# Attention, experts and MLP in one kernel: thresholds on ScalarE and GpSimd, router tables by 108 lanes, steps moved behind the branch

## The chip, the cores and the metric

The kernel runs on one core of a Trainium2 chip. The metric is the device time of one execution in microseconds; the median of several is compared. The core's engines each work off a list of their own: TensorE (PE; its weight loads are shown as PEld), VectorE (DVE), ScalarE (ACT), GpSimd (POOL), and SyncE (SP), which issues most transfers. They wait for one another through semaphores.

## What is computed

Three stages follow one another. Attention has 4 x 8 heads, 576 positions, head width 64, and keeps only scores near each row's maximum. Its output, 2304 tokens of 512, goes to a mixture of 8 experts with one expert per token, and then through an MLP.

```python
    scores = scale * np.matmul(q, k.transpose(0, 1, 3, 2))
    thresh = np.max(scores, axis=-1, keepdims=True) - tau
    scores = np.where(scores >= thresh, scores, -1000000000.0)
    scores = scores - np.max(scores, axis=-1, keepdims=True)
    attn = np.exp(scores)
    attn = attn / (np.sum(attn, axis=-1, keepdims=True) + 1e-09)
    return np.matmul(attn, v).astype(np.float32)
...
    logits = x @ w_gate
    e_idx = np.argmax(logits, axis=1)
...
    eom = 1.0 / (1.0 + np.exp(-(x @ w_output_gate)))
...
        h = np.maximum(x[mask] @ w1[e], 0.0)
        ye = h @ w2[e]
        out[mask] = gate_w[mask, None] * eom[mask, e, None] * ye
...
    h = x @ w_in
    g = np.maximum(0.01 * h, h)
    return (g @ w_out).astype(np.float32)
```

## The kernel before

**Attention** (the first 340 us) works through 16 pairs of heads. A pair P has 9 tiles of 128 rows by 576 columns. Each tile runs: scores on TensorE (L443, into `ps`), row maximum on VectorE (L452, `nm`), then a threshold of one number per row (L456, `th` = tau's share minus `nm`), the exponential on ScalarE (L462, `e`), the mask on VectorE (L470, `em`, which compares the scores with `th`, multiplies with `e` and sums into `rr`), transposes on TensorE (L499, and L535 for the last columns), their evictions (L228 on ScalarE, L230 on VectorE), and the products with the values (AV: L578 in steps of two instructions, L584 as the last step of each half). At a pair's end come L619, L636 and L649 to L651 with the evictions L624, L654 and L662 (`lg`, the gates' logits). For a later pair, GpSimd swaps key halves by DMA (L391, L392) and splits the raw q and k in two parts (casts L290, subtractions L295; `srk`, `srq`), which TensorE transposes (L319, L345). The evictions of a small part of q are `qz`.

**The router** (class `Router`) runs once per batch, that is, after every four pairs: `batch` finds each token's expert (L795 to L821), its rank within the expert (L858 to L880) and its weight (L823 to L846). `choose`, late in attention, picks the expert with most tokens ("star") and makes the list of its first 216 tokens, so that `prefix` can begin its first matrix (L1460) while the last batch is routed. `entries` turns ranks into table entries (`lo`, `sides`): for batches 0 to 2 together after `choose`, for batch 3 alone. `tables` makes the inverse table, the experts' order and the lists of tokens per expert (`gidx`), the flag L1116, and `starts` the first row of each expert.

**The branch.** Each engine loads the flag (L1982) and compares (L1983); the branch body, for experts with more tokens than their window holds, isn't entered with these inputs. Steps that the planner has placed later than `st.t_over` stand behind the branch in each engine's list, the others ahead of it.

**Experts and dense stage.** From 360 us on, eight windows of at most `CAPS` tokens (and the second matrix of the prefix's 216) are computed with weights that arrive by SP's transfers and are split into two parts: casts L1559 and subtractions L1564. L1661 and L1669 and L1675 make the first matrix and its evictions, L1702 the second; L1630 transposes gathered tokens. From 622.9 us the MLP (L1836, L1862) fills TensorE.

The order in each engine's list is made by a list scheduler, `Plan`: each step has an engine (or several to choose from), a cost, a priority and an earliest time, and instructions are put out in planned order. The numbers `st.w_*` are the priorities of the kinds of steps within a pair.

## Time and profile before

| | |
|---|---|
| median of 3 runs | 1031.69 us (1031.01 to 1036.69) |
| profiled execution | 1034.34 us, span 1032.6 us |
| busy share of the span | PE 95%, PEld 81%, DVE 64%, ACT 48%, POOL 25% |
| mean granted TensorE clock | 0.980 of full speed |
| bytes read from and written to HBM | 88.39 MB, 23.31 MB |

A row of a timeline gives start, duration, engine, line, operation, output and inputs with shapes, and in brackets how long the engine stood idle before it, and what released it. A table by stretches gives each engine's busy time within a stretch. A granted clock of 1.00 is TensorE's 2.4 GHz, half of it 1.2 GHz. TensorE's instructions overlap, so what counts is the distance between their starts.

### The profile page before, as it was taken

Reading aid. Unit: us, or ns where it says so; the run is one execution under the profiler, and the core shown is the slowest. Engines: PE = TensorE matmul, PEld = TensorE weight load, DVE = VectorE, ACT = ScalarE, POOL = GpSimd, SP = SyncE. Lnnn points to the kernel's source line nnn. Section 1 sums busy time; section 2 is a strip of 40 time slices with the busy share of each in tenths; the row PEclk is TensorE's granted clock in tenths of the full one; section 3 lists DMA queues with packets and bytes.
Section 4 is the critical chain, followed back from the end, with each engine's and each line's share of the span. In section 5 each row is a group of like instructions: output and inputs, shape, how many; then the busy total and the mean of one; then the engine's idle time right before and its main releaser. Section 6 shows DMA issues by size and latency. Waiting matters only on the chain. (4 is left out here: it accounts for less than half of the span.)

```text
span 1032.6 us, 17029 instructions
## 1 busy us (share of the span) xinstructions
PE 982.6 (95%) x6126; PEld 836.8 (81%) x6126; DVE 658.5 (64%) x1279; ACT 498.0 (48%) x944; POOL 260.2 (25%) x328
## 2 busy tenths in 40 slices
PE   6999999999999799899999999999999999999994
PEld 6777767767776699789999997888888888888884
DVE  7888988898889558998888886533223222322321
ACT  6777767767766255544554644423222322322321
POOL 3533223323211244464337532000100100100000
PEclk9999999999999989899999999999999999999997
DMA  5432423431312597887989877200200200100000
GB/s 140 127 86 71 129 59 85 127 73 41 103 25 96 166 260 261 296 269 241 324 298 320 289 241 232 83 1 12 70 1 1 81 1 1 42 20 1 11 31 22
DMA packets 66876, 122.22 MB, mean 118 GB/s; under 512 B 15776, under 2 KB 33184, under 8 KB 66272
## 3 DMA queue, kind: packets, MB, share of 16 engines
q1 hardware_dynamic: 60368, 100.43, 30.5%
q0 software_dynamic: 6416, 20.63, 7.3%
q8 instruction: 50, 0.82, 0.3%
q14 instruction: 42, 0.34, 0.2%
HBM read 88.39 MB, written 23.31 MB: 108 GB/s over the span
## 5 line engine op out<-in xcount | busy, mean ns | idle before, releaser
L1862 PE MATMUL ps<-arena 128*128 128x512 f32 x864 | 207.4, 390 | 2.3 <-ACT arena L1559 2.3
L1836 PE MATMUL ps<-arena 128*128 128x512 f32 (+1 forms) x960 | 208.1, 368 | 0.0
L1836 PEld LDWEIGHTS ps<-arena 128*128 128x128 f32 x960 | 168.7, 188 | 30.8
L1862 PEld LDWEIGHTS ps<-arena 128*128 128x128 f32 x864 | 161.3, 188 | 35.7 <-ACT arena L1559 2.7
L1847 DVE TENSOR_TENSOR dw<-ps,dw 128x512 f32<-128x512 f32 (+1 forms) x80 | 50.9, 638 | 160.7 <-ACT dw L1843 160.6
L1702 PE MATMUL ps<-arena 128*128 128x216 f32 (+7 forms) x864 | 129.8, 309 | 3.8 <-ACT arena L1669 2.2
L1843 ACT ACTIVATE dw<-ps 128x512 f32<-128x512 f32 (+1 forms) x80 | 44.4, 556 | 183.4 <-PE ps L1836 183.4
L1661 PE MATMUL ps<-arena 128*128 128x400 f32 (+7 forms) x768 | 117.9, 313 | 10.7 <-DVE arena L1675 4.1
L1702 PEld LDWEIGHTS ps<-arena 128*128 128x128 f32 x864 | 124.0, 194 | 4.8 <-ACT arena L1669 2.5
L1661 PEld LDWEIGHTS ps<-arena 128*128 128x128 f32 x768 | 113.9, 194 | 13.6 <-DVE arena L1675 5.1
L452 DVE TENSOR_REDUCE nm<-ps 128x1 f32<-128x576 f32 x144 | 107.0, 753 | 22.4 <-PE ps L443 21.1
L470 DVE SCALAR_TENSOR_TENSOR em<-ps,th,e 128x576 f32<-128x576 f32 x144 | 115.1, 811 | 4.6 <-ACT e L462 2.3
L462 ACT ACTIVATE e<-ps,nm 128x576 f32<-128x576 f32 x144 | 105.7, 749 | 17.0 <-DVE nm L452 12.2
L1891 POOL DMA_INDIRECT out_dram<-sm,oidx x18 | 18.0, 999 | 367.4 <-ACT sm L1885 334.2
L1564 DVE TENSOR_TENSOR arena<-dw,arena 128x512 fp32r<-128x512 f32 (+1 forms) x80 | 52.0, 650 | 91.6 <-PE ps L1862 75.8
L443 PE MATMUL ps<-k,qt 128*128 128x288 f32 x512 | 101.6, 326 | 7.2 <-DVE em L470 6.0
L228 ACT COPY eta<-ps 128x512 f32<-128x512 f32 (+1 forms) x159 | 86.2, 545 | 42.3 <-PE ps L499 41.0
L1559 ACT CAST arena<-raw 128x1024 fp32r<-128x1024 f32 x82 | 84.7, 1048 | 43.1 <-DMA raw<-in_moe_w_dram 33.3
L1564 POOL TENSOR_TENSOR arena<-raw,arena 128x1024 fp32r<-128x1024 f32 x30 | 77.0, 2568 | 82.8 <-ACT arena L1559 69.1
L443 PEld LDWEIGHTS ps<-k,qt 128*128 128x128 f32 x512 | 75.8, 196 | 25.0 <-DVE em L470 10.6
L1564 DVE TENSOR_TENSOR arena<-raw,arena 128x1024 fp32r<-128x1024 f32 x54 | 78.2, 1451 | 26.7 <-ACT arena L1559 21.6
L499 PE MATMUL ps<-ident,em 128*128 128x128 f32 x576 | 89.8, 281 | 1.3 <-DVE em L470 0.7
(236 smaller groups left out, 1161.5 us busy)
## 6 DMA issues: line engine op xcount, KB each, us to landing
raw<-in_moe_w_dram SPq DMA_DIRECT2D x72, 512.0 KB
k<-k POOLq DMA_DIRECT2D x30, 304.0 KB
dw<-in_moe_w_in_dram SPq DMA_DIRECT2D x16, 512.0 KB
wf<-cv SPq DMA_DIRECT2D x32, 256.0 KB
dw<-in_moe_w_out_dram SPq DMA_DIRECT2D x16, 512.0 KB
raw<-wf SPq DMA_DIRECT2D x16, 512.0 KB
rk<-in_k_dram SPq DMA_DIRECT2D x16, 256.0 KB
rq<-in_q_dram SPq DMA_DIRECT2D x16, 256.0 KB
```

The costliest lines, as they stand in the source:

```text
L228: nc.scalar.copy(out=out, in_=in_)
L443: nc.tensor.matmul(out=s[:, c, :], lhsT=lhs, rhs=T[kk, P][:, off + c * HALF:off + (c + 1) * HALF], start=(m == 0), stop=(m == 2 * len(ops) ...
L452: nc.vector.tensor_reduce(out=T["nm", n], in_=T["sc", n], axis=AX.XY, op=ALU.max, negate=True)
L462: nc.scalar.activation(out=T["e", n].rearrange("p (a c) -> p a c", a=2), in_=T["sc", n], func=AF.Exp, bias=T["nm", n][:, 0:1], scale=1.0,)
L470: nc.vector.scalar_tensor_tensor(out=T["em", P, t][:, h, :].rearrange("p (a c) -> p a c", a=2), in0=T["sc", n], scalar=T["th", n][:, 0:1], ...
L499: nc.tensor.transpose(out=bank(o)[:, c * 128:(c + 1) * 128], in_=T["em", P, t][:, h, 64 * h + c * 128:64 * h + (c + 1) * 128], identity=ident,
L1559: nc.scalar.copy(out=out, in_=in_)
L1564: (nc.vector if o.eng == "dve" else nc.gpsimd).tensor_tensor(out=out, in0=in0, in1=in1, op=ALU.subtract)
L1661: nc.tensor.matmul(out=bank(o)[:, 0:n], lhsT=w[:, wi, 128 * f:128 * f + 128], rhs=xx[:, xi, c, :], start=(c == 0 and i == 0), stop=(c == K ...
L1702: nc.tensor.matmul(out=bank(first, d)[:, 0:n], lhsT=w[:, wi, k0:k0 + 128], rhs=hx[:, xi, :], start=(f == 0 and i == 0), stop=(f == 7 and i ...
L1836: nc.tensor.matmul(out=bank(o)[:, 0:n], lhsT=w[:, wi, c, 128 * c2:128 * c2 + 128], rhs=y[:, c, 0:n], start=(k == 0), stop=(k == 3 * KD - 1),)
L1862: nc.tensor.matmul(out=bank(first, t), lhsT=g[:, gi, 128 * t:128 * t + 128], rhs=w[:, wi, c2, :], start=(f == 0 and k == 0), stop=(f == FF ...
```

## The change

1. The thresholds are computed on ScalarE (an activation Identity with scale -1 and tau's share as bias) or on GpSimd; none on VectorE.
2. The tables have 108 lanes (`LANES`) and 6 places for each expert in place of 128 and 4. `entries` runs in every batch: `ge`, `ges`, `lane` and `lo` on VectorE, and `eqj`, `eqab` and two `sides` on GpSimd for batches 0 to 2. The chosen expert's ranks aren't shifted any more; `left` takes its first 216 tokens out of the table at the end. `choose` loses its steps `mine`, `low` and `shift`. Tokens are gathered by 108 rows, 25 gathers in place of 23.
3. The token lists of the experts after the first, the starts and the rest of the last gate come behind the branch; `CAPS[2]` is 324 in place of 336.
4. The planner's numbers are others, and `st.t_over` is 2.2. By the orders of the two kernels, thresholds go from 47 on DVE and 97 on POOL to 85 on ACT and 59 on POOL; 14 of 16 `qz` evictions go from ACT to DVE.

```diff
+LANES = PRE // 2
+
+CAPS = [400, 368, 324, 320, 296, 272, 248, 216]

...
-                (nc.vector if o.eng == "dve" else nc.gpsimd).tensor_tensor(
-                    out=T["th", n], in0=ntau, in1=T["nm", n], op=ALU.subtract
-                )
+                if o.eng == "act":
+                    nc.scalar.activation(out=T["th", n], in_=T["nm", n], func=AF.Identity, bias=ntau[:, 0:1], scale=-1.0)
+                else:
+                    nc.gpsimd.tensor_tensor(out=T["th", n], in0=ntau, in1=T["nm", n], op=ALU.subtract)
...
-            th = pl.add(("dve", "pool"), (0.07, 0.15), thresh, [m], n + st.w_th, label="th")
+            th = pl.add(("act", "pool"), (0.18, 0.15), thresh, [m], n + st.w_th, label="th")
...
-    J = 4
+    J, JW = 6, 4
...
+        entered = self.entries(pl, b, ranked, one_hot, prio)
         if end:
...
+        self.before += entered
...
             nc.vector.tensor_tensor(
-                out=self.lo[:, 5 * b:5 * b + 5, :], in0=self.it.unsqueeze(1).to_broadcast([128, 5, 128]),
-                in1=X["rlo"][:, 5 * (b - b0):5 * (b - b0) + 5].unsqueeze(2).to_broadcast([128, 5, 128]), op=ALU.is_equal,
+                out=ge, in0=rk.unsqueeze(2).to_broadcast([128, 5, J + 1]),
+                in1=self.edge.unsqueeze(1).to_broadcast([128, 5, J + 1]), op=ALU.is_ge,
+            )
+            nc.vector.tensor_reduce(out=s, in_=ge[:, :, 1:J + 1], axis=AX.X, op=ALU.add)
+            nc.vector.scalar_tensor_tensor(out=lane, in0=s, scalar=-float(LANES), in1=rk, op0=ALU.mult, op1=ALU.add)
+
+        def low(o):
+            nc.vector.tensor_tensor(
+                out=self.lo[:, g, :], in0=self.it.unsqueeze(1).to_broadcast([128, 5, 128]),
+                in1=X["lane"].unsqueeze(2).to_broadcast([128, 5, 128]), op=ALU.is_equal,
             )
...
+            V = nc.vector if end else nc.gpsimd
+            eq, ab = w.tile([128, 5, J], F32, name="eqj"), w.tile([128, 5, 2, J], BF16, name="eqab")
...
+        hi = pl.add("dve" if end else "pool", 0.4, high, [pt], prio, label="en")
+        out = [pl.add("dve", 0.8, low, [pt], prio, label="en")]
...
-        m = pl.add("dve", 2.0, mine, [s, ranked], pr, label="ch")
-        ls = [pl.add("dve", 0.8, lambda o, b=b: low(o, b), [m], pr, label="ch") for b in range(NB)]
...
+            self.table(ia_)
+            a, b = t("tsa", (E, J)), self.w.tile([128, E, J], F32, name="tsb")
+            for x, i, m in ((a, 0, self.rest), (b, 2, self.star)):
...
-        a = add("dve", 1.2, lambda o: tokens(o, 1, E), [a])
-        return add("dve", 1.1, starts, [a])
+        self.others, self.starts = lambda o: tokens(o, 1, E), starts
+        return add("dve", 0.9, fits, [a])
...
+    others = pl.add("dve", 1.2, R.others, [], -13, at=free, label="tb")
+    starts = pl.add("dve", 1.3, R.starts, [], 5, at=free, label="tb")
...
-        last = pl.add(eng, cost, f, [last], 6, lat=4.0 if eng == "sp" else 0.0, label="gate")
+        last = pl.add(eng, cost, f, [last], 30, lat=4.0 if eng == "sp" else 0.0, at=20.0, label="gate")
...
-    st.w_s, st.w_m, st.w_th, st.w_x, st.w_kk, st.w_t, st.w_te = -0.39, -0.27, -4.42, -1.71, -7.74, 2.69, -4.82
-    st.w_l = [1.2, 6.62]
...
+    st.w_s, st.w_m, st.w_th, st.w_x, st.w_kk, st.w_t, st.w_te = -0.83, -9.42, -28.19, 3.88, -7.61, 2.26, -14.75
+    st.w_l = [-0.74, 7.52]
...
-    st.t_over = 3.0
...
+    st.t_over = 2.2
```

How the instructions stand now, at the places of which the prediction speaks. First VectorE in the pair that begins the first batch, before: L795 to L805 are steps of the gate's choice, L452 and L470 row maximum and mask.

```order
170 L795 TENSOR_TENSOR scr<-lg 128x160
171 L797 TENSOR_TENSOR lg_1618<-scr 128x80
172 L470 SCALAR_TENSOR_TENSOR em,rr_175<-ps,th,e 128x576
173 L452 TENSOR_REDUCE nm<-ps 128x1
174 L801 TENSOR_REDUCE m<-lg_1618 128x5
175 L456 TENSOR_TENSOR th<-ntau,nm 128x1
176 L805 TENSOR_TENSOR eq<-lg_1618,m 128x40
```

After: L800 to L810 are those steps, L454 and L473 row maximum and mask.

```order
168 L800 TENSOR_TENSOR scr<-lg 128x160
169 L802 TENSOR_TENSOR lg_1621<-scr 128x80
170 L454 TENSOR_REDUCE nm<-ps 128x1
171 L473 SCALAR_TENSOR_TENSOR em,rr_175<-ps,th,e 128x576
172 L806 TENSOR_REDUCE m<-lg_1621 128x5
173 L810 TENSOR_TENSOR eq<-lg_1621,m 128x40
```

The comparison that was L805 is L810 and comes behind one row maximum and one mask, without a threshold in the list.

VectorE in the pair that follows the first batch, before: the threshold L456 and, behind it, the gate's last steps (`og`, `os`, `smr`).

```order
210 L610 TENSOR_SCALAR rr_175<-rr_175 128x10
211 L611 RECIPROCAL rr_175<-rr_175 128x10
212 L452 TENSOR_REDUCE nm<-ps 128x1
213 L470 SCALAR_TENSOR_TENSOR em,rr_173<-ps,th,e 128x576
214 L456 TENSOR_TENSOR th<-ntau,nm 128x1
215 L842 TENSOR_REDUCE smr<-d 128x5
216 L843 TENSOR_SCALAR smr<-smr 128x5
217 L844 TENSOR_SCALAR os<-os 128x5
```

After, the same place: `ge`, `ges`, `lane` and `lo` are the new table steps (L931, L935, L936, L939), L454 and L473 the row maximum and the mask.

```order
204 L931 TENSOR_TENSOR ge<-rk,edge 128x35
205 L935 TENSOR_REDUCE ges<-ge 128x5
206 L936 SCALAR_TENSOR_TENSOR lane<-ges,rk 128x5
207 L657 TENSOR_TENSOR xt<-ps,rr_174 128x128
208 L454 TENSOR_REDUCE nm<-ps 128x1
209 L473 SCALAR_TENSOR_TENSOR em,rr_173<-ps,th,e 128x576
210 L939 TENSOR_TENSOR lo<-it,lane 128x640
211 L828 TENSOR_TENSOR d<-lg_1621,m 128x40
212 L838 TENSOR_TENSOR og<-oh,lg_1621 128x40
```

The threshold is gone from the list; table steps with inputs in SBUF have come into it.

GpSimd in the same pair, before: thresholds, the swap by DMA, and the four operations on raw q and k.

```order
94 L456 TENSOR_TENSOR th<-ntau,nm 128x1 x2
95 L526 COPY em<-em 128x64
96 L456 TENSOR_TENSOR th<-ntau,nm 128x1 x2
97 L391 DMA k_1911<-k_1838 64x1216
98 L392 DMA k_1911<-k_1838 64x1216
99 L290 CAST srk<-rk 128x9x64
100 L290 CAST srq<-rq 128x9x64
101 L295 TENSOR_TENSOR srk<-rk,srk 128x9x64
102 L295 TENSOR_TENSOR srq<-rq,srq 128x9x64
```

After: `eqj`, `eqab` and `sides` are the table steps, L292 and L297 the four operations.

```order
76 L461 TENSOR_TENSOR th<-ntau,nm 128x1 x3
77 L529 COPY em<-em 128x64
78 L393 DMA k_1879<-k_1836 64x1216
79 L394 DMA k_1879<-k_1836 64x1216
80 L948 TENSOR_TENSOR eqj<-ge 128x30
81 L949 TENSOR_TENSOR eqab<-eqj,tt 128x60
82 L955 TENSOR_TENSOR sides<-oh,eqab 128x5x48 x2
83 L292 CAST srk<-rk 128x9x64
84 L292 CAST srq<-rq 128x9x64
85 L297 TENSOR_TENSOR srk<-rk,srk 128x9x64
86 L297 TENSOR_TENSOR srq<-rq,srq 128x9x64
```

The table steps stand directly between the swap and the four operations.

TensorE's list within a pair, before: transposes (L499, L535), AV steps (L578, L584), scores (L443).

```order
457 L499 MATMUL ps<-ident,em 128x128 x4
458 L584 MATMUL ps<-etl,vt_177 128x288
459 L578 MATMUL ps<-eta,rv 64x288 x4
460 L443 MATMUL ps<-k_1561,qt 128x288
461 L443 MATMUL ps<-k_1637,qt 128x288
462 L443 MATMUL ps<-k_1561,qt 128x288
463 L443 MATMUL ps<-k_1637,qt 128x288
464 L499 MATMUL ps<-ident,em 128x128 x4
465 L578 MATMUL ps<-eta,rv 64x288 x4
466 L535 MATMUL ps<-ident,em 128x128 x3
467 L584 MATMUL ps<-etl,vt_177 128x288
468 L443 MATMUL ps<-k_1561,qt 128x288
```

After, the same stage of a pair (L502, L538 transposes, L581, L587 AV, L445 scores).

```order
450 L502 MATMUL ps<-ident,em 128x128 x4
451 L581 MATMUL ps<-eta,rv 64x288 x4
452 L445 MATMUL ps<-k_1565,qt 128x288
453 L445 MATMUL ps<-k_1602,qt 128x288
454 L445 MATMUL ps<-k_1565,qt 128x288
455 L445 MATMUL ps<-k_1602,qt 128x288
456 L502 MATMUL ps<-ident,em 128x128 x4
457 L581 MATMUL ps<-eta,rv 64x288 x2
458 L587 MATMUL ps<-etl,vt_177 128x288
459 L445 MATMUL ps<-k_1565,qt 128x288
460 L445 MATMUL ps<-k_1602,qt 128x288
461 L445 MATMUL ps<-k_1565,qt 128x288
```

The AV steps stand in smaller groups, more of them behind transposes.

VectorE's list at the end of the last batch, before: the flag (L1116), then the other tokens (L1103 to L1108) and the starts (L1120 to L1124).

```order
565 L1116 TENSOR_SCALAR flag<-mcap 128x1
566 L1103 TENSOR_TENSOR scr<-one,tab 128x224
567 L1107 TENSOR_REDUCE tk_4651<-scr 128x28
568 L1108 TENSOR_SCALAR gidx<-tk_4651 128x28
569 L1120 TENSOR_TENSOR scr<-gt,cnt 128x64
570 L1121 TENSOR_REDUCE off<-scr 128x8
571 L1122 TENSOR_SCALAR off<-off 128x8
572 L1064 TENSOR_TENSOR scr<-one,off 128x64
573 L1065 TENSOR_REDUCE offr<-scr 128x8
574 L1124 CAST offi<-offr 128x8
```

After: the flag is L1087, and L1958, L1959 are the load of the flag and the branch.

```order
582 L1085 TENSOR_TENSOR dcap<-cnt,cap 128x8
583 L1086 TENSOR_REDUCE mcap<-dcap 128x1
584 L1087 TENSOR_SCALAR flag<-mcap 128x1
585 L1958 TENSOR_LOAD flag
586 L1959 COMPARE_AND_BRANCH
```

And behind the branch's body, which ends with an unconditional branch, the tokens (L1074 to L1079) and the subtraction (L1538, L1564 before):

```order
723 L1959 UNCONDITIONAL_BRANCH x2
724 L1074 TENSOR_TENSOR scr<-one,tsa 128x224
725 L1078 TENSOR_REDUCE tk_7059<-scr 128x28
726 L1079 TENSOR_SCALAR gidx<-tk_7059 128x28
727 L1651 SCALAR_TENSOR_TENSOR arena<-ps,arena 128x216 x2
728 L1538 TENSOR_TENSOR arena<-raw_66,arena 128x1024
```

The branch has come directly behind the flag, and the tokens and the subtraction behind the branch.

## Rows read from the trace of the kernel before

**Rows 1.** Table by stretches: span, length, busy us by engine, PEclk, DMA share, GB/s.

```profile
100.00:120.00 20.00, 20.00 (x156) 15.07 (x153) 17.55 (x45) 15.38 (x32) 7.08 (x15) 1.00 0.45 136
120.00:140.00 20.00, 17.55 (x133) 13.94 (x132) 19.50 (x47) 12.76 (x29) 7.43 (x12) 0.94 0.33 84
280.00:340.00 60.00, 56.24 (x460) 42.33 (x459) 52.62 (x141) 37.01 (x80) 11.87 (x38) 1.00 0.18 55
360.00:380.00 20.00, 18.39 (x118) 17.73 (x119) 12.89 (x22) 9.13 (x17) 12.04 (x7) 0.76 0.90 210
```

**Rows 2.** Timeline of PE around the first router batch and one pair later.

```profile
123.67 0.43 PE L636 MATMUL ps<-xu,gd 128*32 128x128 f32 x8
...
137.25 1.16 PE L443 MATMUL ps<-k,qt 128*128 128x288 f32 x4 [2.31 <-DVE em L470]
...
147.78 0.43 PE L636 MATMUL ps<-xu,gd 128*32 128x128 f32 x8
...
167.17 0.42 PE L636 MATMUL ps<-xu,gd 128*32 128x128 f32 x8
```

**Rows 3.** Timeline of DVE around the first router batch.

```profile
120.31 1.11 DVE L816 TENSOR_TENSOR oh<-eq,fm 128x40 bf16<-128x40 f32 x1
...
131.68 4.01 DVE L456 TENSOR_TENSOR th<-ntau,nm 128x1 f32<-128x1 f32 x1
```

**Rows 4.** Timeline of POOL, 129 to 138 us.

```profile
131.65 0.70 POOL L290 CAST srk<-rk 128x576 fp32r<-128x576 f32 x1
...
134.25 1.41 POOL L295 TENSOR_TENSOR srq<-rq,srq 128x576 fp32r<-128x576 f32 x1
```

**Rows 5.** L456 on DVE: ns min/median/max; then its group: busy us, mean ns.

```profile
L456 DVE TENSOR_TENSOR th<-ntau,nm x47: 147/159/4007, 15.0 to 276.9; 128x1 f32<-128x1 f32 x47
...
L456 DVE TENSOR_TENSOR th<-ntau,nm 128x1 f32<-128x1 f32 x47 | 16.8, 362 | 0.6
```

**Rows 6.** Instruction groups of ACT: busy us, mean ns of one.

```profile
L838 ACT ACTIVATE os<-os 128x5 f32<-128x5 f32 x4 | 0.9, 213 | 0.0
```

**Rows 7.** Timeline of DVE in the last router batch.

```profile
344.63 0.82 DVE L930 TENSOR_TENSOR lo<-it,rlob 128x640 bf16<-128x640 int32 x1
...
345.82 0.32 DVE L948 TENSOR_TENSOR sides<-oh,eqabb 128x160 bf16<-128x160 bf16 x1
```

**Rows 8.** Timeline of PE in a plain pair.

```profile
159.85 0.60 PE L499 MATMUL ps<-ident,em 128*128 128x128 f32 x4
160.21 0.77 PE L443 MATMUL ps<-k,qt 128*128 128x288 f32 x4
160.91 0.71 PE L578 MATMUL ps<-eta,rv 128*64 128x288 f32 x4
161.55 0.66 PE L499 MATMUL ps<-ident,em 128*128 128x128 f32 x4
162.14 1.19 PE L578 MATMUL ps<-eta,rv 128*64 128x288 f32 x8
163.26 0.75 PE L584 MATMUL ps<-etl,vt 128*128 128x288 f32 x2
```

**Rows 9.** Timeline of DVE before the branch.

```profile
349.92 0.15 DVE L1116 TENSOR_SCALAR flag<-mcap 128x1 int32<-128x1 f32 x1
...
354.30 1.23 DVE L1564 TENSOR_TENSOR arena<-raw,arena 128x1024 fp32r<-128x1024 f32 x1 [1.31 <-ACT arena L1559]
```

**Rows 10.** L1983, the branch, on the queue of DVE: ns, first and last start.

```profile
L1983 DVEq EVENT_SEMAPHORE  x1: 21/21/21, 359.4 to 359.4; - x1
```

**Rows 11.** Timeline of PE at three places of the expert stage.

```profile
361.56 0.76 PE L1702 MATMUL ps<-arena 128*128 128x216 f32 x2 [1.05 <-DVE arena L1675]
...
377.50 2.72 PE L1661 MATMUL ps<-arena 128*128 128x400 f32 x14
...
417.44 0.67 PE L1661 MATMUL ps<-arena 128*128 128x368 f32 x1 [3.58 <-ACT arena L1559]
```

**Rows 12.** Instruction groups of PE.

```profile
L1702 PE MATMUL ps<-arena 128*128 128x336 f32 x96 | 15.5, 319 | 0.0
```

More of the change, by code (lines that the diff above doesn't have):

```diff
@@ L717, in __init__ @@
         self.first = c.tile([128, 2], I32, name="first")
-        self.less = c.tile([128, 1], F32, name="less")
+        self.rest = c.tile([128, E], F32, name="rest")
         self.far = c.tile([128, NB, 5], I32, name="far")
@@ L761, in consts @@
         nc.vector.memset(self.oh, 0.0)
[L762 to L763 removed]
+        nc.vector.tensor_scalar(
+            out=self.edge, in0=self.it[:, 0:self.J + 1], scalar1=float(LANES), scalar2=None, op0=ALU.mult
+        )
         nc.vector.memset(self.far, 0)
@@ L951, in side @@
             )
         pt = pl.add("dve", 0.6, parts, [ranked], prio, label="en")
-        out = [pl.add("dve", 0.8, lambda o, b=b: low(o, b), [pt], prio, label="en") for b in range(b0, b1)]
-        hi = pl.add("dve", 0.45, high, [pt], prio, label="en")
-        for b in range(b0, b1):
-            for a in range(2):
-                out.append(pl.add(
-                    "dve" if end and a == 0 else "pool", 0.35 if end and a == 0 else 0.55, lambda o, b=b, a=a: side(o, b, a),
-                    [hi, one_hot], prio, label="en"))
@@ L961, in entries @@
-        return out
-    def choose(self, pl, ranked, prio):
-        nc, E, w, st, NB = self.nc, self.E, self.wt, self.st, self.G // 5 - 1
+        hi = pl.add("dve" if end else "pool", 0.4, high, [pt], prio, label="en")
+        out = [pl.add("dve", 0.8, low, [pt], prio, label="en")]
+        for a in range(2):
+            dve = end and a == 0
+            out.append(pl.add("dve" if dve else "pool", 0.4 if dve else 0.65, lambda o, a=a: side(o, a), [hi, one_hot], prio, label="en"))
+        return out
@@ new lines, in inverse, with table @@
+    def inverse(self, o, g0, g1, a, n):
+        nc, E, J = self.nc, self.E, self.J
+        for g in range(g0, g1):
+            nc.tensor.matmul(
+                out=self.st.ps[:, a.slots[self.st.bk][0], 0:2 * E * J], lhsT=self.lo[:, g, :],
+                rhs=self.sides[:, g].rearrange("p a e j -> p (a e j)"), start=(g == 0), stop=(g == n - 1),
+            )
+    def table(self, a):
+        V, n, tab = self.nc.vector, self.E * self.J, self.tab.rearrange("p e j -> p (e j)")
+        inv = self.st.ps[:, a.slots[self.st.bk][0], 0:2 * n]
+        V.tensor_scalar(out=tab, in0=inv[:, 0:n], scalar1=256.0, scalar2=-1.0, op0=ALU.mult, op1=ALU.add)
+        V.tensor_tensor(out=tab, in0=inv[:, n:2 * n], in1=tab, op=ALU.add)
@@ L1011, in low @@
-        def low(o, b):
-            V.tensor_tensor(
-                out=self.lo[:, 5 * b:5 * b + 5, :], in0=self.it.unsqueeze(1).to_broadcast([128, 5, 128]),
-                in1=X["rlo"][:, 5 * b:5 * b + 5].unsqueeze(2).to_broadcast([128, 5, 128]), op=ALU.is_equal,
-            )
-        def mm(o):
-            for g in range(n):
-                nc.tensor.matmul(
-                    out=st.ps[:, o.slots[bk][0], 0:4], lhsT=self.lo[:, g, :], rhs=X["ab"][:, g].rearrange("p a j -> p (a j)"),
-                    start=(g == 0), stop=(g == n - 1),
-                )
@@ L1085, in ids, with left @@
             V.tensor_copy(out=self.eidi, in_=self.eid)
-        def inverse(o, g0, g1, a):
-            for g in range(g0, g1):
-                nc.tensor.matmul(
-                    out=st.ps[:, a.slots[bk][0], 0:2 * n], lhsT=self.lo[:, g, :], rhs=self.sides[:, g].rearrange("p a e j -> p (a e j)"),
-                    start=(g == 0), stop=(g == G - 1),
-                )
-        def tab(o):
-            inv, ia = st.ps[:, ia_.slots[bk][0], 0:2 * n], t("ia", (n,))
-            V.tensor_scalar(out=ia, in0=inv[:, 0:n], scalar1=256.0, scalar2=-1.0, op0=ALU.mult, op1=ALU.add)
-            V.tensor_tensor(out=self.tab.rearrange("p e j -> p (e j)"), in0=inv[:, n:2 * n], in1=ia, op=ALU.add)
+        def left(o):
+            self.table(ia_)
+            a, b = t("tsa", (E, J)), self.w.tile([128, E, J], F32, name="tsb")
+            for x, i, m in ((a, 0, self.rest), (b, 2, self.star)):
+                V.tensor_tensor(
+                    out=x, in0=self.tab[:, :, i:i + J], in1=m.unsqueeze(2).to_broadcast([128, E, J]), op=ALU.mult
+                )
+            V.tensor_tensor(out=a, in0=a, in1=b, op=ALU.add)
+            self.ts = a
         def tokens(o, r0, r1):
@@ L1232, in overs @@
         self.piece = t
+        self.starts(None)
         steps, mm, last = self.rows()
@@ L1776, in experts @@
     for i, (eng, cost, f) in enumerate(steps):
-        done.append(pl.add(eng, cost, lambda o, f=f: f(), done if eng == "pool" else done[:1], 100 + 4 * i, at=60.0, label="rows"))
+        done.append(pl.add(eng, cost, lambda o, f=f: f(), done if eng == "pool" else done[:1] or [starts], 100 + 4 * i, at=60.0, label="rows"))
     a = pl.add("pe", 1.3, lambda o: mm_rows(o.slots[bk][0]), done, 140, acq=[(bk, 1), (r_tp, 1)], label="rows")
```

171 lines of the change are left out of this document (68 added, 103 removed).

## The prediction

> **What bounds the kernel now.** I read the table by stretches first, for the engines side by side. In attention TensorE is busy 20.00 us of every 20 where nothing goes wrong (100 to 120), VectorE 17.55 and ScalarE 15.38, so that TensorE's own order of issue sets the pace; in 120 to 140 it loses 2.45 us, and there VectorE is at 19.50 [rows 1]. Then I took the pace from one instruction that comes once per head pair (L636): it starts at 123.67, 147.78 and 167.17 us [rows 2]. A plain pair takes 19.39 us, the one with the router's first batch 24.11, so 4.72 more. VectorE's list in that stretch gives the reason: one threshold of L456, 128x1, took 4.01 us, from 131.68 to 135.69 [rows 3], where the median of its kind is 0.159 [rows 5], and in just that time GpSimd ran two casts and two subtractions one behind the other, the first starting at 131.65, the last ending at 135.66 [rows 4]. TensorE then stood 2.31 us for a mask [rows 2]. The 47 thresholds take 16.8 us together; 45 at the median make 7.2, and what is left has room for two of 4.0 [rows 5], the second in the router's second batch. So an operation of VectorE whose two inputs lie in SBUF can wait out GpSimd's whole run.
>
> **Thresholds off VectorE.** Removed: 45 thresholds at 0.159, 7.2 us, or 0.45 per pair, and the two of 4.0 [rows 5]. Added: 85 on ScalarE and 59 on GpSimd, which had 97. The nearest row there, an activation on 128x5, has 213 ns [rows 6], so 85 x 0.213 = 18.1 us, 1.1 us per pair. ScalarE goes from 15.4 to about 16.5 of 20, and gives back a little with 14 qz evictions that go to VectorE: no bound, so cost nothing. What hides it is the time in which ScalarE waits for TensorE's and VectorE's results; without that cover it would be 1.1 us per pair.
>
> **What stands where the thresholds stood.** Taking the stalled threshold away saves 4.7 us per batch only if no other operation with two SBUF inputs meets GpSimd's run. The order of the changed kernel shows two that do, in batches 0 and 1 alike. First, in the pair that begins the batch: GpSimd's four operations start when the row maximum ahead of the mask is done, and VectorE comes, behind that mask and a small reduction (about 1 us), to L810, a comparison of two SBUF tiles. Such a run lasts 4.0 us [rows 4], so L810 would wait some 3.2. A row of before shows this very place: L816, an operation of the same kind and size two steps later, took 1.11 us at 120.31, about 0.9 more than it needs [rows 3]. Second, in the next pair the new table steps eqj, eqab and sides (four operations of 30, 60, 240 and 240 elements; from VectorE's 0.32 for 160 elements in L948 [rows 7] I estimate 1.3 us together) stand on GpSimd right ahead of the four, a run of 5.3 us that starts when `ge` is done. Behind `ge` VectorE has `lane` (two SBUF inputs), a row maximum, a mask and `lo` (0.82, two SBUF inputs [rows 7]). If `lane` slips in ahead, `lo` waits about 2.9 us; if not, `lane` waits 5.
>
> Price: the block of 3.85 us became 4.72 us of the pair, 1.2 per us, TensorE's half clock behind its idle time included (0.94 granted in 120 to 140, against 1.00 in the stretch before [rows 1]). So 3.2 x 1.2 = 3.9 and 2.9 to 5 x 1.2 = 3.5 to 6.0: 7.4 to 9.9 per batch, against 4.7 and 0.9 x 1.2 = 1.1 before, 5.8. That is +1.6 to +4.1 per batch, +3.2 to +8.2 for two; without any meeting it is -11.6. Batch 2 lies where GpSimd has no such run left, and I put it at 0; in 280 to 340 TensorE loses 3.76 of 60 us [rows 1], which is the end that follows. Taken: +5, since the caught L456 and L816 are the nearest rows. The page "SBUF — State Buffer" of the Trainium skill, section "Who interferes with whom", says that a VectorE instruction with two SBUF inputs contends with a GpSimd one that reads SBUF, and that the first to issue holds the port for one whole instruction; by that, no wait could pass one GpSimd instruction. The trace disagrees on the length: 4.01 us over four instructions, of which the first took 0.70 and the last 1.41 [rows 3, 4]. By the page's length the two waits would be at most 1.4 each.
>
> **The order on TensorE.** The planner's numbers are new, and with them the order of all pairs. Counted over the orders, the AV steps (L578, now L581) stand in 97 groups instead of 85, 41 directly behind transposes instead of 25, and 4 instead of 13 behind the last AV step; score groups go from 124 to 137. Starts of groups give the prices [rows 8]: two AV steps (four instructions) 0.64 from 160.91, four steps 1.12 from 162.14, so a split costs 0.16; AV starts 0.59 after the transposes of 161.55, scores 0.36 after those of 159.85, so 0.23 more; the 9 groups that no longer follow an AV step give back up to 0.2 each, and a score group more I put at 0.1, both estimates by the 0.16 and 0.23. 12 x 0.16 + 16 x 0.23 - 9 x 0.2 + 13 x 0.1 = 5.1 us over the 15 pairs that this reaches, 0.34 per pair. Bounds +2 (the extra groups hide where VectorE is late anyway) to +9 (all 16 at 0.23 and every group at the dearer prices). Taken +5.
>
> **End of attention.** The tables of batches 0 to 2 no longer come together: twice three `lo` at 0.82 [rows 7] and the small steps around them, between 5 and 9 us of VectorE near 320 to 336, go to the batches and become one `lo` each. TensorE lost 3.76 us in 280 to 340 [rows 1]: -1.5, between 0 and -3.76.
>
> **Late steps behind the branch.** Before, VectorE has the flag at 350.07 (349.92 + 0.15), but computes the other tokens, the starts and three gate steps first, waits 1.31 us for a cast of ScalarE and subtracts until 355.53 [rows 9]; its queue is through the branch at 359.4 [rows 10], 3.9 us after that. The full second matrices start at 361.56 [rows 11]. In the order of the changed kernel the load of the flag stands right behind the flag. The flag itself comes some 0.5 us later (three products in `left`, each below L948's 0.32 [rows 7], less a shorter chain ahead). With the same 3.9 us, VectorE goes on at 350.6 + 3.9 = 354.5, and not before the engines that join the branch are there, so near 355.5 to 356; then it owes the tokens (three operations, which I estimate at 1.1 by L948's 0.32 and `lo`'s 0.82 [rows 7]) and the subtraction (1.23), so the matrices run from about 358.5. What is late next is ScalarE, whose two casts ahead of the branch stay, or the weights of the next window, whose first matmul is at 377.50 [rows 11]. Taken -4.5: 3 us at the start, plus 1.5 of the 4.8 us that the half clock costs behind it (0.76 granted in 360 to 380, 0.24 of 20 us [rows 1]); bounds -1 (weights late) and -7. The gate's puts, which SP issued in the midst of that stretch, go to the planner's 20 us and later; the loads that they meet there are inside those bounds.
>
> **Caps and experts.** CAPS[2] 336 to 324 shortens 192 matmuls of L1661 and L1702: 96 of them at 336 columns take 15.5 us [rows 12], 12 columns less give 15.5 x 12/336 = 0.55, twice: -1.0. Two gathers more on GpSimd lie beside TensorE's work. The stall of 3.58 us at 417.44, where ScalarE's eviction of a window's last tokens came late [rows 11], has a new order around it that moves one weight load ahead of a store: 0, with -4.5 to +4. The dense order is the same: 0.
>
> **Sum** on the profiled execution, 1034.34 (span 1032.6): +5 batches, +5 order, -1.5 end, -4.5 branch, -1.0 caps = +3.0, 1037.3. The median of runs, 1031.69, lies 2.65 lower: 1034.7.
>
> **Rivals.** (1) Slower: `lane` itself is caught and the order costs its upper price: batches +8.2, order +9, the rest -7: +10.2, 1042. For it: in a plain pair TensorE has no idle time that could hide a dearer order; against: VectorE has 2.45 of 20 us to spare. It decides from 3 us of wait per batch more than before. (2) Faster: nothing is caught, since GpSimd starts its run earlier or lets VectorE in between two instructions: -11.6 in place of +5, 1018. For it: every plain pair has such a run and no stall; against: the 4.01. The page's rule of one instruction leads here too: waits of 1.4 stay within the 1.5 us that the block of 3.85 had to spare over TensorE's 2.31. (3) The r1 stall goes too and the branch gives 7: 1034.7 - 7 = 1027.7. (4) The change at the branch doesn't do what it says, because weights or ScalarE's casts set the end: 1038.2.
>
> **Chances.** Forecast 0.42, (1) 0.22, (2) 0.17, (3) 0.11, (4) 0.08. A measurement here can tell about 0.5% from no change, 5.2 us. Faster by more: (2), half of (3), a little of the forecast's spread: 0.27. Slower by more: (1), (4) and a part of the forecast's: 0.35. Within: 0.38. Both signs hold over half together, so the forecast's own range: 1029 to 1040. The whole range reaches to (2) and a little past (1): 1018 to 1044.
>
> **What would show it.** In the profile after: L810 and `lo` or `lane` (L936, L939) with some us in the first 240 us, and the two batch pairs at 23 us or more by the starts of L639, which is L636 now; plain pairs at 19.6 to 19.9 instead of 19.39; the first matmul of the 400-token window near 373 instead of 377.5. It is wrong if those steps keep their fractions of a us (then rival 2), or if plain pairs stay at 19.39 (then 5 us less).

## The result and the profile after

The kernel after takes 1019.21 us (median of 4, 1017.89 to 1020.83), the kernel before 1031.35 (median of 4, 1028.69 to 1036.69) in the same comparison: ratio 0.9877, interval 0.9834 to 0.9919, so 1.2% faster. The same two kernels, measured again on the chip of e5 to e8 and on that of e9 to e12, gave 0.9933 (0.9904 to 0.9962) and 0.9910 (0.9881 to 0.9939). The forecast was 1034.7, no change; the nearest of its cases is the rival "nothing is caught" with 1018.

The span went from 1032.6 to 1019.1 us. Where the 13.5 us lie, by the starts of instructions that stand in both traces (before: L636, L1116, L1702, L1661, L1836; after: L639, L1087, L1678, L1637, L1812):

| stretch | before | after | difference |
|---|---|---|---|
| start to the first pair's output (L636) | 46.0 | 46.87 | +0.9 |
| from there 14 pairs on | 283.49 | 275.36 | -8.1 |
| to the flag | 20.43 | 21.23 | +0.8 |
| flag to the first second matrix | 10.03 | 6.23 | -3.8 |
| to the first matrix of the second window (368 tokens) | 57.49 | 58.70 | +1.2 |
| to the second matrix of the third window (336, now 324) | 56.79 | 53.36 | -3.4 |
| to the dense stage | 148.68 | 149.52 | +0.8 |
| dense stage | 409.65 | 407.78 | -1.9 |

The 14 pairs hold two things of opposite sign. First the table by stretches of the kernel after (columns as in [rows 1]).

```profile
100.00:120.00 20.00, 20.00 (x154) 14.72 (x152) 17.48 (x43) 14.32 (x32) 6.12 (x11) 1.00 0.44 135
120.00:140.00 20.00, 19.82 (x160) 15.66 (x161) 19.09 (x52) 17.45 (x43) 8.22 (x14) 1.00 0.30 77
280.00:340.00 60.00, 59.01 (x477) 45.91 (x476) 47.41 (x139) 36.63 (x83) 10.78 (x30) 1.00 0.26 84
340.00:360.00 20.00, 14.34 (x83) 13.39 (x83) 12.37 (x36) 8.06 (x16) 6.05 (x6) 0.83 0.66 209
400.00:420.00 20.00, 13.00 (x62) 12.40 (x61) 18.49 (x28) 10.19 (x17) 10.49 (x5) 0.83 0.98 352
```

TensorE now has 19.82 of 20 us in the first batch's stretch at a clock of 1.00, where it had 17.55 at 0.94 [rows 1]. Its timeline at the instruction that marks a pair (L639, L636 before):

```profile
125.50 0.43 PE L639 MATMUL ps<-xu,gd 128*32 128x128 f32 x8
...
145.38 0.43 PE L639 MATMUL ps<-xu,gd 128*32 128x128 f32 x8
...
165.19 0.42 PE L639 MATMUL ps<-xu,gd 128*32 128x128 f32 x8
```

The pair with the batch takes 19.88 us (24.11 in [rows 2]), the plain one behind it 19.81 (19.39). VectorE's timeline shows what the prediction expected to be caught: L810, `lane` (L936) and `lo` (L939).

```profile
113.05 0.20 DVE L810 TENSOR_TENSOR eq<-lg,m 128x40 f32<-128x40 f32 x1
...
115.78 1.37 DVE L816 TENSOR_TENSOR eq<-eq,desc 128x40 f32<-128x40 f32 x1
...
130.64 0.17 DVE L936 SCALAR_TENSOR_TENSOR lane<-ges,rk 128x5 f32<-128x5 f32 x1
...
132.91 0.90 DVE L939 TENSOR_TENSOR lo<-it,lane 128x640 bf16<-128x640 int32 x1
133.73 0.66 DVE L828 TENSOR_TENSOR d<-lg,m 128x40 f32<-128x40 f32 x1
```

And GpSimd's runs at those two places:

```profile
112.41 0.66 POOL L292 CAST srk<-rk 128x576 fp32r<-128x576 f32 x1
113.67 0.67 POOL L292 CAST srq<-rq 128x576 fp32r<-128x576 f32 x1 [0.60 <-PE ps L321]
114.30 1.41 POOL L297 TENSOR_TENSOR srk<-rk,srk 128x576 fp32r<-128x576 f32 x1
115.68 1.42 POOL L297 TENSOR_TENSOR srq<-rq,srq 128x576 fp32r<-128x576 f32 x1
...
132.47 0.66 POOL L292 CAST srk<-rk 128x576 fp32r<-128x576 f32 x1
133.07 1.26 POOL L292 CAST srq<-rq 128x576 fp32r<-128x576 f32 x1
134.30 1.48 POOL L297 TENSOR_TENSOR srk<-rk,srk 128x576 fp32r<-128x576 f32 x1
```

The first run isn't one piece: its second cast waited 0.60 us for TensorE, and L810 went through in that gap. L816 met the last operation alone (115.68 to 117.10) and lost 1.17 us. `lane` slipped in ahead of the second run. `lo` came in its midst and still took only 0.90; here it was GpSimd that waited, whose next cast took 1.26 in place of 0.67. `d` (L828) then lost 0.47 us behind that cast. VectorE so loses some 1.7 us per batch: L816's 1.17 in the pair ahead of the batch pair (105.68 to 125.50, 19.82 us), the rest in the batch pair (19.88). Both are within 0.1 us of 19.81, the pair without a batch. The places are the ones forecast; the waits are not.

Behind the branch, the lists of VectorE and TensorE:

```profile
343.46 0.15 DVE L1087 TENSOR_SCALAR flag<-mcap 128x1 int32<-128x1 f32 x1
349.24 0.57 DVE L1074 TENSOR_TENSOR scr<-one,tsa 128x224 f32<-128x224 f32 x1 [5.63 <-DVEq L1959]
```

```profile
349.69 0.37 PE L1678 MATMUL ps<-arena 128*128 128x216 f32 x1 [0.32 <-ACT arena L1645]
351.57 0.55 PE L1678 MATMUL ps<-arena 128*128 128x216 f32 x1 [1.51 <-DVE arena L1651]
352.99 2.47 PE L1678 MATMUL ps<-arena 128*128 128x216 f32 x10 [0.88 <-DVE arena L1538]
...
408.39 0.46 PE L1637 MATMUL ps<-arena 128*128 128x368 f32 x1 [4.84 <-ACT arena L1533]
411.01 18.15 PE L1637 MATMUL ps<-arena 128*128 128x368 f32 x95 [2.16 <-DVE arena L1538]
```

Second matrices in a row start 9.5 us behind the flag (352.99 - 343.46) in place of 11.6 (361.56 - 349.92 [rows 9, 11]), and the first matrix of the 400-token window 23.60 us behind it in place of 27.58. The wait at the second window, 3.58 in [rows 11] and another 0.90 one instruction later, is 4.84 and another 2.16 now.

### The profile page after: what moved, and what is told of

Same layout as the page of the kernel before. It is cut to its first block, busy times and chain, and to the rows that moved or that the text cites. A ratio compares the mean times of both kernels' runs of the same rounds, so it can differ in the third digit from the quotient of the medians.

```text
span 1019.1 us, 17026 instructions
## 1 busy us (share of the span) xinstructions
PE 974.4 (96%) x6134; PEld 830.4 (81%) x6134; DVE 640.2 (63%) x1255; ACT 511.0 (50%) x1017; POOL 245.4 (24%) x293
## 5 line engine op out<-in xcount | busy, mean ns | idle before, releaser
L1812 PE MATMUL ps<-arena 128*128 128x512 f32 (+1 forms) x960 | 208.1, 368 | 0.0
L1812 PEld LDWEIGHTS ps<-arena 128*128 128x128 f32 x960 | 168.7, 188 | 30.8
L1678 PE MATMUL ps<-arena 128*128 128x216 f32 (+7 forms) x864 | 127.7, 306 | 2.7 <-DVE arena L1651 1.5
L1637 PE MATMUL ps<-arena 128*128 128x400 f32 (+7 forms) x768 | 114.8, 309 | 13.9 <-DVE arena L1651 6.1
L1678 PEld LDWEIGHTS ps<-arena 128*128 128x128 f32 x864 | 122.0, 192 | 3.5 <-DVE arena L1651 1.7
L1637 PEld LDWEIGHTS ps<-arena 128*128 128x128 f32 x768 | 111.4, 191 | 15.6 <-DVE arena L1651 7.0
L454 DVE TENSOR_REDUCE nm<-ps 128x1 f32<-128x576 f32 x144 | 108.5, 754 | 21.3 <-PE ps L445 17.7
L473 DVE SCALAR_TENSOR_TENSOR em<-ps,th,e 128x576 f32<-128x576 f32 x144 | 115.9, 805 | 1.6 <-ACT e L465 1.4
L1538 DVE TENSOR_TENSOR arena<-dw,arena 128x512 fp32r<-128x512 f32 (+1 forms) x80 | 51.2, 640 | 93.0 <-PE ps L1838 78.7
L445 PE MATMUL ps<-k,qt 128*128 128x288 f32 x512 | 102.2, 323 | 1.7 <-ACT qt L236 0.9
L445 PEld LDWEIGHTS ps<-k,qt 128*128 128x128 f32 x512 | 73.6, 188 | 32.2 <-DVE em L473 8.3
L230 ACT COPY eta<-ps 128x512 f32<-128x512 f32 (+1 forms) x157 | 83.4, 543 | 24.4 <-PE ps L502 24.2
L1538 DVE TENSOR_TENSOR arena<-raw,arena 128x1024 fp32r<-128x1024 f32 x59 | 81.0, 1382 | 17.1 <-ACT arena L1533 17.0
L502 PE MATMUL ps<-ident,em 128*128 128x128 f32 x576 | 85.0, 275 | 1.4 <-DVE em L473 1.4
L581 PE MATMUL ps<-eta,rv 128*64 128x288 f32 x512 | 83.8, 425 | 0.6 <-ACT k L230 0.5
```

The costliest lines, as they stand in the source:

```text
L445: nc.tensor.matmul(out=s[:, c, :], lhsT=lhs, rhs=T[kk, P][:, off + c * HALF:off + (c + 1) * HALF], start=(m == 0), stop=(m == 2 * len(ops) ...
L454: nc.vector.tensor_reduce(out=T["nm", n], in_=T["sc", n], axis=AX.XY, op=ALU.max, negate=True)
L473: nc.vector.scalar_tensor_tensor(out=T["em", P, t][:, h, :].rearrange("p (a c) -> p a c", a=2), in0=T["sc", n], scalar=T["th", n][:, 0:1], ...
L502: nc.tensor.transpose(out=bank(o)[:, c * 128:(c + 1) * 128], in_=T["em", P, t][:, h, 64 * h + c * 128:64 * h + (c + 1) * 128], identity=ident,
L581: nc.tensor.matmul(out=out[64 * h:64 * h + 64], lhsT=T["rv", P][:, 4 * h + c, :], rhs=T["eta", P][:, h, c, lo_:lo_ + HALF], start=(c == 0) ...
L1538: (nc.vector if o.eng == "dve" else nc.gpsimd).tensor_tensor(out=out, in0=in0, in1=in1, op=ALU.subtract)
```

## The experiments

Each compares with the trace of before or of after. A "pair" is the distance between two starts of L636 or its successor. The fifth, the ninth and the thirteenth of these distances hold the work of a router batch and are called batch pairs; the others from the second to the twelfth are the plain pairs.

**Thresholds off VectorE alone.** The order of before, the 47 thresholds on ScalarE.

```diff
-                (nc.vector if o.eng == "dve" else nc.gpsimd).tensor_tensor(
-                    out=T["th", n], in0=ntau, in1=T["nm", n], op=ALU.subtract
-                )
+                if o.eng == "dve":
+                    nc.scalar.activation(out=T["th", n], in_=T["nm", n], func=AF.Identity, bias=ntau[:, 0:1], scale=-1.0)
+                else:
+                    nc.gpsimd.tensor_tensor(out=T["th", n], in0=ntau, in1=T["nm", n], op=ALU.subtract)
```

> Kernel before, with its own order; only the 47 thresholds that VectorE computed are an activation on ScalarE, at the same places. Theory of the prediction (an operation of VectorE with two SBUF inputs waits out GpSimd's whole run of four): the gate's small steps behind the threshold (L844 to L850 here) are caught in its place, the pairs with the first two batches stay near 23 to 24 us, time within 3 us of before. Rival A (a wait of that kind ends with one GpSimd instruction, and the two of 4.01 us are a special meeting): those two pairs fall from 24.1 to at most 20 us, time 8 to 10 us below before.

Ratio to before 0.9983 (0.9956 to 1.0011): no change that can be told. The pairs of the first two batches took 22.77 us each. VectorE's and TensorE's timelines of this kernel:

```profile
129.88 0.19 DVE L843 TENSOR_REDUCE smr<-d 128x5 f32<-128x40 f32 x1
130.11 3.81 DVE L844 TENSOR_SCALAR smr<-smr 128x5 f32<-128x5 f32 x1
133.83 0.16 DVE L845 TENSOR_SCALAR os<-os 128x5 f32<-128x5 f32 x1
```

```profile
135.17 0.81 PE L443 MATMUL ps<-k,qt 128*128 128x288 f32 x4 [2.03 <-DVE em L471]
```

The reduction passed, and the next step with its input in SBUF waited in the threshold's place, to the end of GpSimd's four operations (129.84 to 133.88). It has one input in SBUF, not two: the condition in the prediction was too narrow. So here the prediction's mechanism holds, and point 1 of the change by itself is worth little in the old order.

**A small operation ahead of the two stalled thresholds.**

```diff
+                if n in (56, 92):
+                    gap = sm_p.tile([128, 192], F32, tag="gap", name="gap")
+                    nc.vector.memset(gap, 0.0)
                 (nc.vector if o.eng == "dve" else nc.gpsimd).tensor_tensor(
```

> Kernel before; only ahead of the two thresholds that took 4.01 us stands one fill of a 128x192 tile on VectorE (0.1 to 0.3 us), so that each comes that much later into GpSimd's run. Theory of the prediction: it waits for what is left of the run, about 3.7 us, and the pair stays at 24 us. Rival A, with the moment of arrival as the special thing (the threshold came 0.03 us after the run began): it waits at most 0.6 us, and the pair falls to about 20 us.

The threshold came 0.24 us into the run in place of 0.03 and waited to its end all the same:

```profile
130.01 0.22 DVE L458 MEMSET gap<- 128x192 f32 x1
130.15 3.81 DVE L459 TENSOR_TENSOR th<-ntau,nm 128x1 f32<-128x1 f32 x1
```

Batch pairs 22.82 and 23.94; 1036.98 us in one run, with before at 1035.39 on that chip. The moment of arrival at the run's start isn't what makes it long; rival A in that form falls.

**The held steps.** e1's kernel, with the gate's last five steps of the first two batches put five masks later.

```diff
-        step("dve", 0.6, s8)
-        step("sp", 0.5, put, lat=4.0)
+        step("dve", 0.6, hold if b < 2 else s8)
+        step("sp", 0.5, held_put, lat=4.0)
...
+                if getattr(st, "held", None):
+                    st.held[0] -= 1
```

> Kernel of e1_th_off (thresholds off VectorE in the order of before), and in the first two batches the gate's last five steps (L842 to L846 of before) come on VectorE five masks later, out of GpSimd's run. In e1_th_off it was the second of these that waited 3.81 us in the threshold's place. Theory now (whoever stands first in the run with SBUF inputs waits, and the pair pays 3.4 us for 3.8 of wait and 1.3 more where the clock falls): no such wait is left there, the two pairs fall from 22.77 to 19.4 to 20, time 6 to 7 us below e1_th_off. Rival (the router's own work on VectorE makes the pairs long): they stay above 22.

The pairs fell to 20.20 and 20.20 (the one behind each is 19.81, 0.43 more than a plain one). TensorE's marks in this kernel:

```profile
123.91 0.42 PE L643 MATMUL ps<-xu,gd 128*32 128x128 f32 x8
...
144.11 0.43 PE L643 MATMUL ps<-xu,gd 128*32 128x128 f32 x8
```

With nothing left in the run, 22.77 of e1 (24.11 in before) becomes 20.20, a little above the 19.4 to 20 expected: this shows that the caught operation made most of what the batch pairs were longer by. The router's own work is what stays, 0.82 there and 0.43 in the pair behind. In time, 1031.40 against 1035.93 for before on the same chip (0.9961, 0.9932 to 0.9989); the 6 to 7 us below e1 that I expected can't be compared in time, since e1 ran on another chip. In the traces, the flag comes 296.98 us behind the first pair's output (343.30 - 46.32) in place of e1's 301.26 (345.50 - 44.24), 4.3 us less; two pairs less 2.57 each, plus 0.43 each for the next, make the same 4.3. So the 6 to 7 us were too much.

**Thresholds back on VectorE in the order of after.**

```diff
-                    nc.scalar.activation(out=T["th", n], in_=T["nm", n], func=AF.Identity, bias=ntau[:, 0:1], scale=-1.0)
+                    nc.vector.tensor_tensor(out=T["th", n], in0=ntau, in1=T["nm", n], op=ALU.subtract)
```

> Kernel after, with its own order; only the 85 thresholds on ScalarE are a subtraction on VectorE again, at the same places. Theory of the prediction: wherever one meets a run it waits for the rest of it, up to 4 us, so several pairs grow by up to 4.7 us each, and the time by 10 us or more. Rival A: waits end at one instruction, at most 1.4 us; VectorE gets 85 x 0.16 = 13.6 us, 0.9 per pair, within its idle time; time within 5 us of the kernel after.

1043.17 us in one run, with before at 1035.39 on that chip. Most plain pairs are 20.36 (after 19.81), the first pair's output comes at 53.28 (46.87), and the batch pairs take 22.27 and 20.74. The group of thresholds on VectorE, then two of them in its timeline and GpSimd's timeline at these two:

```profile
L459 DVE TENSOR_TENSOR th<-ntau,nm 128x1 f32<-128x1 f32 x85 | 29.6, 349 | 0.3
```

```profile
35.43 3.22 DVE L459 TENSOR_TENSOR th<-ntau,nm 128x1 f32<-128x1 f32 x1
...
61.71 1.36 DVE L459 TENSOR_TENSOR th<-ntau,nm 128x1 f32<-128x1 f32 x1
```

```profile
35.24 1.43 POOL L297 TENSOR_TENSOR srk<-rk,srk 128x576 fp32r<-128x576 f32 x1
36.61 1.41 POOL L297 TENSOR_TENSOR srq<-rq,srq 128x576 fp32r<-128x576 f32 x1
37.95 0.67 POOL L292 CAST srk<-rk 128x576 fp32r<-128x576 f32 x1
...
61.63 1.41 POOL L297 TENSOR_TENSOR srk<-rk,srk 128x576 fp32r<-128x576 f32 x1
63.01 1.40 POOL L297 TENSOR_TENSOR srq<-rq,srq 128x576 fp32r<-128x576 f32 x1
```

Both outcomes in one kernel: the threshold at 35.43 waited out three operations, the one at 61.71 got in behind the first although another followed at once. So "waits out the run" and "waits out one instruction" are each wrong as a rule. The first batch pair shows what waits in a row cost:

```profile
141.85 1.35 DVE L939 TENSOR_TENSOR lo<-it,lane 128x640 bf16<-128x640 int32 x1
143.12 1.40 DVE L828 TENSOR_TENSOR d<-lg,m 128x40 f32<-128x40 f32 x1
144.45 1.43 DVE L838 TENSOR_TENSOR og<-oh,lg 128x40 f32<-128x40 bf16 x1
```

The three lose 0.5, 1.2 and 1.2 us, `d` getting in behind one operation although another followed, and TensorE then stands 1.54 us for a mask in that pair of 22.27. And point 1 of the change, worth little in the old order, is worth some 16 to 22 us of span in the new one (1041.4 against 1019.1 to 1025.5, on different chips). In most pairs one threshold meets GpSimd's run (1.32 us in seven of them), and TensorE stands 0.48 us for a mask in most plain pairs; how much of the 16 to 22 us is waits and how much the thresholds' own time on VectorE (85 at about 0.16 us, 13.6 us) isn't separated.

**A probe in the run.**

```diff
+            if P in (4, 8):
+                pb = sm_p.tile([128, 1], F32, tag="pb", name="pb")
+                one = ntau if P == 4 else bank(a)[:, 160:161]
+                nc.vector.tensor_tensor(out=pb, in0=one, in1=T["g", P][:, 0:1] if P == 4 else ntau, op=ALU.subtract)
```

> Kernel after with two probes on VectorE, one 128x1 subtraction each, behind the eviction L657 in the pairs where GpSimd's run begins with the table steps eqj, eqab and sides: in the pair of batch 0 with two SBUF inputs, in that of batch 1 with one input in PSUM. Theory of the prediction: the first waits until the run's end, 5 to 6 us, and its pair grows by some 6 us; the second takes 0.15 to 0.2. Rival A: the first waits at most 0.6 us (one sides) and the pair stays within 0.7 us of 19.89; the second is the same.

Neither waited: 149 and 146 ns (1029.42 us in one run). The trace shows why that decides nothing: the probe ran from 130.82 to 130.97, between `eqj` (to 130.83) and `eqab` (from 130.91), and these table steps have gaps, since each waits for the one before. It only shows that my "run of 5.3 us" began with a stretch that isn't closed.

**Lists and starts ahead of the branch again**, in the kernel after.

```diff
-        self.others, self.starts = lambda o: tokens(o, 1, E), starts
-        return add("dve", 0.9, fits, [a])
+        self.starts = starts
+        a = add("dve", 0.9, fits, [a])
+        self.made = add("dve", 1.2, lambda o: tokens(o, 1, E), [a])
+        return add("dve", 1.3, starts, [self.made])
...
-    others = pl.add("dve", 1.2, R.others, [], -13, at=free, label="tb")
-    starts = pl.add("dve", 1.3, R.starts, [], 5, at=free, label="tb")
+    others = starts = None
...
-    st.t_over = 2.2
+    st.t_over = 3.0
```

> Kernel after, but the lists of the other experts' tokens and the starts stand ahead of the branch again (about 2.5 us of VectorE), and the planner's limit for the branch is 3.0 as before. Prediction's step (each us ahead of the branch on VectorE's list delays the second matrices): from the flag to the first second matrix takes 8 to 10 us in place of after's 6.2, and the expert stage begins 2 to 4 us later. Rival (other engines, SP or GpSimd, set when the branch is passed): it stays within 1 us of 6.2.

In this kernel the flag and the first second matrix are at

```profile
344.19 0.15 DVE L1087 TENSOR_SCALAR flag<-mcap 128x1 int32<-128x1 f32 x1
...
346.65 0.17 DVE L1095 CAST offi<-offr 128x8 int32<-128x8 f32 x1
```

```profile
352.87 0.55 PE L1679 MATMUL ps<-arena 128*128 128x216 f32 x1 [1.10 <-ACT arena L1646]
```

so 8.68 us lie between them. In three traces of the kernel after it is 6.23, 6.64 (e8, the same chip) and 6.90 (e12): 1.8 to 2.45 more, for the 2.55 us from 344.27 to 346.82 that VectorE works there. So most of each us ahead of the branch on VectorE is paid, and the rival's 1 us is passed. Of the 3.8 us gained, these steps are 1.8 to 2.45; the rest I did not take apart. In time, one run at 1031.28 against a median of 1028.42 for after on that chip (1020.94 to 1030.81).

**The order of the pairs.** Four kernels, the one after with lines of the planner's numbers from before: all five lines of a pair's steps (e5), `w_s` to `w_te` (e9), these with `w_l` and `w_av` (e10), `w_xo` (e11). The edit of e9:

```diff
-    st.w_s, st.w_m, st.w_th, st.w_x, st.w_kk, st.w_t, st.w_te = -0.83, -9.42, -28.19, 3.88, -7.61, 2.26, -14.75
+    st.w_s, st.w_m, st.w_th, st.w_x, st.w_kk, st.w_t, st.w_te = -0.39, -0.27, -4.42, -1.71, -7.74, 2.69, -4.82
```

> Kernel after, but with the planner's numbers for the steps within a pair from the kernel before (w_k, w_s to w_te, w_l, w_av, w_xo); thresholds, tables and late steps as in after. Its order has 78 groups of AV steps (97 in after, 85 in before), 30 of them right behind transposes (40, 23). If the price of a plain pair, 19.81 in after against 19.38 in before, comes from such groups, plain pairs fall to 19.2 to 19.5, 4 to 6 us in all; unless VectorE meets GpSimd's run again, the time lies some 5 us below after. If the price comes from something else (ScalarE's thresholds, say), plain pairs stay near 19.8 and the time within 2 us of after.

> Kernel after with one line of the planner's numbers from before (w_s to w_te, the priorities of scores, maximum, threshold, exponential, mask, transposes). Its order has 79 groups of AV steps, 19 of them behind transposes (after 97 and 40). By the starts of groups read in the trace of before, its plain pairs would take 0.6 us less than after's. If TensorE's order sets the pair: 19.2 to 19.4 in place of 19.81, some 5 to 8 us in all below after on the same chip. Rival (the new priorities kept VectorE's small steps out of GpSimd's run): batch pairs over 21 and no gain.

> Kernel after with three lines of the planner's numbers from before (w_s to w_te, w_l, w_av and d_av): 78 groups of AV steps, 28 behind transposes, 127 groups of scores (after 137). By the same sum the cheapest order on TensorE, 9 us less than after's over attention. If TensorE's order alone sets the pace, 7 to 10 us below after; if the router's batches meet GpSimd's run again, up to 4.7 us more for each batch.

> Kernel after with w_xo alone from before (when a pair's output goes out): 81 groups of AV steps, 29 behind transposes. By the sum 7 us less than after's on TensorE. The same two readings as for e10_prio3.

> The kernel after itself, for comparison on the same chip: plain pairs 19.8, the first two batch pairs 19.9, time 10 to 14 us below before.

> The kernel after itself, for comparison with these three on the same chip: plain pairs 19.8, batch pairs 19.9, time 7 to 13 us below before.

| kernel | groups of AV steps | plain pairs, us | batch pairs, us | time, median us | after on the same chip |
|---|---|---|---|---|---|
| after | 97 | 19.49 to 19.84 | 19.88, 19.88, 19.92 | | |
| e5 | 78 | 19.38 to 21.55 | 19.62, 20.32, 22.70 | 1031.26 | 1028.42 |
| e9 | 79 | 19.15 to 20.23 | 21.42, 20.96, 19.85 | 1024.66 | 1022.59 |
| e10 | 78 | 19.15 to 21.20 | 21.11, 21.12, 20.62 | 1027.72 | 1022.59 |
| e11 | 81 | 18.10 to 22.10 | 20.19, 21.21, 20.41 | 1024.47 | 1022.59 |

Two plain pairs of e9, on TensorE:

```profile
149.32 0.42 PE L639 MATMUL ps<-xu,gd 128*32 128x128 f32 x8
...
168.47 0.43 PE L639 MATMUL ps<-xu,gd 128*32 128x128 f32 x8
```

19.15 us with fewer groups, as the price by groups would have it. That it is the groups isn't shown: that line of numbers moves other steps too, and the pair of e9 from 187.65 to 207.37 has as many groups of AV steps in the trace, no idle time of TensorE, and takes 19.72. In e5 and e11 single pairs are no prices either, since eight instructions of a pair's end can fall into the next distance (18.10 and 21.39 follow one another in e11).

None of the four beats the kernel after, so the gains of 5 to 10 us that I expected didn't come; e9 and e11 lie within the range of after's own runs on their chip (1020.12 to 1027.44). Each gives the gain back in other pairs (20 to 22 us). Part of that is idle time of TensorE, 1.8 us in e9's first batch pair and 0.33 in its plain pairs of 20.23. The rival's signs for e9 came, batch pairs about 21 and no gain, and in the first of them a small step of VectorE with one SBUF input again waited in GpSimd's run:

```profile
138.72 1.28 DVE L613 TENSOR_SCALAR rr<-rr 128x10 f32<-128x10 f32 x1
```

TensorE's order alone isn't what sets the sum; that of after is dearer per pair and nearly the same from pair to pair. e8 came out 7.5 us below before, less than the 10 to 14 expected, and e12 10.4.

## Why the prediction was wrong

**Right.** The plain pair: 5.1 us over 15 pairs forecast, 0.34 each; measured 19.81 against 19.38, 0.43 each, in most of them. That the groups are the reason is argued, not shown. The branch: -4.5 forecast (3 at the start of the matrices, 1.5 of clock); measured -2.1 at the start of the matrices in a row and -4.0 up to the first matrix of the 400-token window, and e6 shows the mechanism. ScalarE hides its thresholds, at 297 ns each in place of the 213 taken: with 47 of them there, e1's plain pairs stay at 19.37. That thresholds alone bring little in the old order, since the next step is caught: e1.

**The step that failed** is "What stands where the thresholds stood": I took +5 us for the router's first two batches, and they gave -9.2 (4.72 and 4.63 us over a plain pair before, 0.1 each after). It failed in three places. First, the run: I took GpSimd's four operations as one closed piece wherever the order has them in a row. The order says nothing of waits, and in the first pair the second cast waited for TensorE, which let L810 through; in e4 the table steps ahead of the second run weren't closed either. Second, the wait: I made a rule of "until the run ends" from one row and its like. Six instances in before, e1 and e2 followed it, and one of e3; but `lo` and `d` in after, `d` in e3 and the threshold of 61.71 in e3 got in behind one operation. The page "SBUF — State Buffer" of the Trainium skill, section "Who interferes with whom", has the lock held for one whole instruction, and I read it so that a wait ends there; the latter rows agree with that, the seven others don't, and what tells them apart stays open. Third, the price: I took 1.2 us of pair per us of wait in proportion from the first us on. But waits within VectorE's spare time cost next to nothing: in after, 1.2 us in one pair and 0.5 in the next cost 0.1 at most. I had that number, 1.5 us to spare, and used it only for the rival. Before showed it too: L816's 0.9 us [rows 3], which I priced at 1.1, lies in a pair of 19.37 us, as long as its neighbours (it ends at 123.67 [rows 2] and begins here):

```profile
104.30 0.43 PE L636 MATMUL ps<-xu,gd 128*32 128x128 f32 x8
```

Rival 2 had this mechanism, with a chance of 0.17. It named the wrong reason in part: GpSimd let VectorE in, but the run also had gaps of its own. That its 1018 lies so near is partly luck: its -11.6 was for two batches, which gave -9.2, and the third batch, at 0 in every case, gave another -2.8.

**Also mis-sized:** batch 2 (0 taken, -2.8 measured: the pair was 22.27 and is 19.92). The end of attention, -1.5 taken, came to +0.8 up to the flag: VectorE's list is shorter (47.41 us busy in 280 to 340 in place of 52.62), and the gain seems to lie in batch 2's pair, and not behind it. The list alone doesn't bring it: e5, with the same tables and steps in another order, has 22.70 in that pair. Experts and dense stage: -1.0 taken for caps and 0 for the rest; measured -3.3 (+1.2 - 3.4 + 0.8 - 1.9). The second window's stall grew by 2.5 us, that at the third window's first matrix fell from 2.30 to 0.74, and that at the start of the dense second matrix from 2.28 to 0.33. I didn't test these one by one.

## What to carry to other kernels

When one operation is caught behind another engine's work, look at what stands next in the list: moving the caught operation alone can do no more than change which one waits. Price a wait against the spare time of its engine first, and only the rest as lost time. An order of instructions shows neighbours, not gaps: whether a row of operations runs closed depends on waits that only a trace shows.
